# GateLoop and a low-rank mixer on one core: up products of two pairs ahead of the mix instead of one, with stacked float32r corrections

## The chip, the cores and the metric

The kernel runs on one core of a Trainium2 chip. The metric is the device time of one execution in microseconds (us): the median of several runs, and for the profile the time of the one execution that was profiled. TensorE is called PE, VectorE DVE, ScalarE ACT, GpSimd POOL and SyncE SP, as in the profile.

## The reference

```python
# attention: B, H, S, D = 4, 8, 768, 48; all inputs float32
for t in range(S):
    new_re = ar * S_re - ai * S_im          # ar, ai: the gate a[t], its magnitude cut at 0.999
    new_im = ar * S_im + ai * S_re
    S_re, S_im = new_re + k[t] (outer) v[t], new_im
    y[t] = q[t] @ S_re
x = y as (B, S, H * D)                      # (4, 768, 384)
# mixer: U (768, 32), V (32, 768), w_ch1 (384, 1536), w_ch2 (1536, 384)
h = x.transpose(0, 2, 1) @ U @ V            # a sum over the 768 tokens of a batch
u = x + h.transpose(0, 2, 1)                # "the mix"
out = u + relu(u @ w_ch1) @ w_ch2           # "up", then "down"
```

The weights of the mixer arrive as 64-bit floats and are converted on the chip.

## The kernel before, in words

**Work and order.** The 3072 tokens are 24 chunks of 128 tokens, six to a batch; two chunks are a pair, so there are 12 pairs (`m` = 0 to 11), three to a batch. Every operation is first entered in a plan (`PE(...)`, `ACT(...)`, `DVE(...)`, `POOL(...)`, `SP(...)`) with a planner's cost, what it reads and writes, and the buffers it takes. What is then issued is a list written out by hand or by a search, `ORDER`: the plan's operation numbers in one common order, from which each engine gets its own queue, in order. `SPARE` gives, for some operation numbers, how many dummy products PE makes just ahead of that operation (two records each). SP issues the loads and small transfers, POOL the stores of finished outputs and the carries between chunks.

**The chunks.** `gates` turns the gate inputs of two chunks at a time into magnitudes and angles (`magnitudes`, `turns`, `waves`; ACT and DVE, with prefix sums as PE products at lines 750 to 820). `prep` weighs q and k, forms the `QKC` tiles and transposes them on PE (line 881); `chain` makes a chunk's products (910, 930, 968, 960), carries the state `G` from chunk to chunk, and leaves the chunk's part of x in `xo`.

**The mixer of a pair.** The function `mixer(m)` does, when a batch is complete, the rank product `rank` (line 1003: x times U, summed over the six chunks, 32 columns wide, in four quarters of 96 columns on four groups of 32 partitions), its copy `r` (1009), and per pair: `spread` (line 1063: 16 tiled products with V on 32 rows each) and `mixed` (1070: four additions onto `xo`), `turned` (transposes of u), up, and down.

**Two forms of up.** `up_cut` is used from pair 1 on. Weights and inputs are cut into a high part and a low part (`cut_weights`, once; `turned`, per pair), and each block of outputs is made of three kinds of float32r products: high with high, low with low (lines 1148, 1150) and the crossed differences (1155), the last added by DVE (1169). `up` (line 1179) makes plain float32 products. It is used for pair 0 with `ahead`: that is, from x before the mix, as soon as the pair's two chunks are there. The part that the mix would have added is corrected later: `ranked` (line 1196) multiplies the transposed r with w_ch1 into `rws`, and `corrected` (lines 1214, 1220) multiplies that with V in tiles of 32 rows and adds it to h with the relu.

**Three forms of down.** `down` for pair 0 (line 1243), `down_two` for pairs 1 to 8 (line 1286; seven products instead of eight, each in two halves of three), `down_three` for the last three pairs (1463).

**Constants.** `AHEAD = 1` counts the pairs whose up is made ahead; `THREE = 9` and `PLAIN = 1` choose the forms of down. `weights` loads the weights in pieces of 768 KB through two staging buffers (`raw`); a piece below `EARLY` has its two conversions on DVE, a later one on ACT.

Of the kernel before, what the change touches and what calls it, by code (L numbers as in the profile page):

```python
# [10 lines left out]
FP = mybir.dt.float32  # L11
# [105 lines left out]
)  # L117

SPARE = {
    110: 8, 133: 7, 137: 2, 194: 3, 198: 2, 201: 3, 208: 1, 218: 5, 247: 5, 409: 2, 548: 1, 2206: 14,  # L120
}

DUMP = None
# [1562 lines left out]
```

## Time and profile before

| what | value |
|---|---|
| runs | 533.96, 535.43, 535.63 us; median 535.43 |
| the profiled execution | 535.18 us; its span from first to last instruction 533.3 us |
| granted PE clock | 1.0 throughout |
| PE busy | 511.0 us (96%) |
| DVE busy | 430.7 us (81%) |
| ACT busy | 310.5 us (58%) |
| DMA | 39.92 MB; mean 75 GB/s, 163 to 225 GB/s in the first seven of 40 slices of the span |

Busy time of PE is modelled from pipelined products, so a product that waits may look busy; "PEld", the loading of weights into PE, shows the gaps better. A line of the chain of waits reads: start in us, duration in us, engine, tile, line, number of instructions. A line of a group of instructions reads: line, engine, operation, output and inputs, shapes, count, then busy us and mean ns of one, then idle time of the engine ahead of them.

### The profile page before, as it was taken

What the parts mean: (1) busy time and instruction counts of PE and PEld (TensorE: products, weight loads), DVE (VectorE), ACT (ScalarE), POOL (GpSimd) and SP (SyncE); (2) the same over time, 40 slices, a digit from 0 to 9 for tenths busy, and PEclk for the clock granted to TensorE, in tenths of its full rate; (3) what the DMA queues carried; (4) which work ended last, traced back from release to release, by engine and by line L of the source; (5) the groups of instructions that cost most, each with busy time, mean ns of one, the idle gap of its engine ahead of it and who ended that gap; (6) DMA issues with size and microseconds to landing.
All of it is one profiled execution on the core that took longest, in us unless ns stands there. A gap on an engine that the chain in (4) does not pass through costs nothing.

```text
span 533.3 us, 17003 instructions
## 1 busy us (share of the span) xinstructions
PE 511.0 (96%) x7454; PEld 466.5 (87%) x7454; DVE 430.7 (81%) x798; ACT 310.5 (58%) x554; POOL 29.9 (6%) x57
## 2 busy tenths in 40 slices
PE   7789999899999998999999999999999999999996
PEld 7567686469999988999999989999999899999996
DVE  7998999999998976886977866786967758788741
ACT  6879999777587783655568764453475652321000
POOL 1000000000102000011002000011002000000020
PEclk9999999999999999999999999999999999999999
DMA  9996968430254442303217460024104300000011
GB/s 185 206 214 163 225 166 197 87 60 1 39 85 105 92 97 29 61 30 69 45 32 128 79 121 17 16 40 91 31 3 85 62 12 2 1 1 1 0 64 52
DMA packets 150704, 39.92 MB, mean 75 GB/s; under 512 B 145880, under 2 KB 147440, under 8 KB 150624
## 3 DMA queue, kind: packets, MB, share of 16 engines
q1 hardware_dynamic: 148544, 34.63, 33.1%
q0 software_dynamic: 2080, 4.15, 2.3%
q8 instruction: 59, 0.97, 0.8%
q14 instruction: 21, 0.17, 0.1%
HBM read 33.60 MB, written 4.76 MB: 72 GB/s over the span
## 4 chain that ended last, share of the span: by engine, by line
PE 79%; DVE 10%; ACT 6%; issue 2%; DMA 1%; SPq 0%; ACTq 0%; DVEq 0%
PE down L1286 20%; PE up L1148 8%; PE bank L1155 8%; PE up L1150 8%; PE bank L1463 7%; PE bank L910 4%; PE bank L881 4%; PE bank L968 4%; PE bank L930 3%; PE bank L960 3%; PE down L1243 2%; PE up L1179 2%; PE bank L1063 1%; PE bank L814 1%; DMA qk<-in_q_dram 1%
## 5 line engine op out<-in xcount | busy, mean ns | idle before, releaser
L1148 PE MATMUL up<-uh,wh 128*128 128x256 f32 x396 | 70.6, 287 | 0.1
L1150 PE MATMUL up<-ul,wl 128*128 128x256 f32 x396 | 68.5, 281 | 0.3 <-DVE ul L1107 0.3
L461 ACT ACTIVATE h<-up 128x512 f32<-128x512 f32 x60 | 35.2, 594 | 46.8 <-PE up L1150 46.3
L1148 PEld LDWEIGHTS up<-uh,wh 128*128 128x128 f32 x396 | 56.8, 189 | 1.2 <-ACT h L461 0.3
L1150 PEld LDWEIGHTS up<-ul,wl 128*128 128x128 f32 x396 | 56.2, 189 | 0.5 <-DVE ul L1107 0.5
L887 ACT COPY QK<-bank 112x512 f32<-112x512 f32 x96 | 51.2, 590 | 8.8 <-PE bank L881 8.6
L1155 PE MATMUL bank<-ud,wd 128*128 128x256 f32 x396 | 55.2, 283 | 0.0
L1286 PE MATMUL down<-w,h 128*128 128x192 f32 x288 | 53.6, 331 | 0.2
L1155 PEld LDWEIGHTS bank<-ud,wd 128*128 128x128 f32 x396 | 50.7, 188 | 0.2
L464 DVE TENSOR_TENSOR QKC<-qk,cs 128x768 f32<-128x768 f32 x48 | 44.9, 955 | 5.8 <-ACT cs L461 4.0
L1286 PEld LDWEIGHTS down<-w,h 128*128 128x128 f32 x288 | 46.6, 190 | 1.5 <-DVE h L1169 0.4
L467 DVE TENSOR_TENSOR xo<-bank,xo 128x192 f32<-128x192 f32 x78 | 26.1, 354 | 24.3 <-PE bank L1463 17.5
L1169 DVE CUSTOM_DVE_ANT_0 h<-bank,h 128x512 f32<-128x512 f32 x54 | 35.8, 687 | 10.2 <-PE bank L1155 8.1
L1286 PE MATMUL down<-stage 128*128 128x192 f32 x192 | 35.7, 333 | 0.5 <-issue 0.3
L800 POOL DMA_DIRECT2D z<-F x15 | 12.1, 806 | 376.1 <-ACT z L461 102.9
L1286 PEld LDWEIGHTS down<-stage 128*128 128x128 f32 x192 | 31.0, 190 | 1.6 <-issue 0.4
L458 ACT ACT_TABLE_LOAD x24 | 30.8, 1283 | 1.1 <-PEq L1670 0.7
L881 PE MATMUL bank<-ident,QKC 64*112 64x64 f32 x768 | 28.5, 220 | 2.4 <-DVE QKC L464 1.7
L881 PEld LDWEIGHTS bank<-ident,QKC 64*112 64x112 f32 x768 | 24.1, 130 | 7.5 <-issue 2.6
L1106 ACT CAST uh<-low 128x384 fp32r<-128x384 f32 x22 | 11.2, 509 | 31.2 <-DVE low L1104 26.6
L910 PE MATMUL bank<-QK 112*64 112x64 f32 x768 | 27.6, 225 | 0.6 <-ACT QK L887 0.6
L910 PEld LDWEIGHTS bank<-QK 112*64 112x64 f32 x768 | 24.3, 138 | 3.9 <-issue 1.7
(234 smaller groups left out, 1066.4 us busy)
## 6 DMA issues: line engine op xcount, KB each, us to landing
stage<-in_moe_w_ch_dram SPq DMA_DIRECT2D x12, 768.0 KB
qk<-in_q_dram SPq DMA_DIRECT2D x24, 192.0 KB
qk<-in_k_dram SPq DMA_DIRECT2D x24, 192.0 KB
values<-in_v_dram SPq DMA_DIRECT2D x24, 192.0 KB
gate<-in_a_re_dram SPq DMA_DIRECT2D x22, 192.0 KB
gate<-in_a_im_dram SPq DMA_DIRECT2D x22, 192.0 KB
out_dram<-xo POOLq DMA_DIRECT2D x13, 192.0 KB, 3.0
out_dram<-xo POOLq DMA_DIRECT2D x16, 96.0 KB, 3.1
```

Of the source, the lines that this page charges most:

```text
L458: ACT(1.4, rank, lambda: nc.scalar.preload_act_table_set(name), writes=[TABLE])
L461: return nc.scalar.activation(out=o, in_=i, func=f, **kw)
L464: nc.vector.tensor_tensor(out=o, in0=a, in1=b, op=OP.mult)
L881: nc.tensor.transpose(out=get(*ps[r])[0:DQ, h], in_=get(*qkc)[at, h].rearrange("p u d -> p (u d)")[:, 0:DQ], identity=ident[at, at], tile_ ...
L887: nc.scalar.copy(out=get(*QK)[0:DQ, u].rearrange("p (h t) -> p h t", t=CH)[:, :, r * HC:(r + 1) * HC], in_=get(*ps[r])[0:DQ])
L910: nc.tensor.matmul(out=get(*ps0)[r:r + HC, h], lhsT=k_of(h, r, HC), rhs=q_of(h, r, HC), start=True, stop=True, tile_position=(0, r))
L1148: nc.tensor.matmul(out=get(*X)[:, e], lhsT=get("wh", f)[:, at(e)], rhs=get(*uh)[:, f], start=(f == 0), stop=False)
L1150: nc.tensor.matmul(out=get(*X)[:, e], lhsT=wl_of(f)[:, at(e)], rhs=get(*ul)[:, f], start=False, stop=(f == KD - 1))
L1155: nc.tensor.matmul(out=get(*Y)[:, e], lhsT=wd[:, f, at(e)], rhs=get(*ud)[:, f], start=(f == 0), stop=(f == KD - 1))
L1169: DVE(c_dve(2 * N), R0, lambda: nc.vector._custom_dve(dve_ops.TENSOR_ADD_SAT, out=where_(), in0=get(*Y), in1=where_(), s0=math.inf, s1=0.0 ...
L1286: nc.tensor.matmul(out=get(*to)[:, part], lhsT=x(j), rhs=y[:, j], start=(first and j == 0), stop=(j == KH - 1), skip_group_check=not first)
L1463: nc.tensor.matmul(out=get(*ps), lhsT=w[0]()[:, q], rhs=x[0]()[:, q], start=(n == 0 and q == 0), stop=(q == k3 - 1), skip_group_check=True)
```

## The change

**Pairs.** `AHEAD` becomes 2 and a new constant `CUTS = 2` says from which pair on up is made in the cut form. Pairs 0 and 1 both get plain float32 up products from x before the mix, and corrections. `cut_weights` and `turned` in its cut form come in with pair 2. h of pair 0 takes the space that later holds the low weights (`wl`), h of pair 1 the usual one; the tiles `wd` and V share their space in time with the new operands.

**Stacked corrections.** V is held a second time as `V4`, a float32r tile of 128 rows: four copies of its 32 rows, of which the second and the fourth hold what float32r rounding left over. r is sent to DRAM and back into four places of 32 partitions (`low`), with all 384 columns, and made into `R4`: the first two groups rounded, the last two the remainder. One product of 128 rows then gives the sum of four partial products. `spread` becomes one float32r product of 384 columns for each chunk, `mixed` one addition of 384 columns. In the same way `rws` goes to DRAM and back and becomes `rw4`, and `corrected` becomes two float32r products and one addition of 512 columns for each two blocks of h, six times a pair.

**The rest.** U and V are loaded as the sixth piece instead of the third, and the pieces with conversions on DVE are 0, 3, 4, 5 and 6; `QKC` loses its gap between the two halves' paddings; the five constant columns share one tile; from batch 1 on, r's quarters are cut as contiguous columns. `ORDER` is another list (2231 operations instead of 2208), and `SPARE` has 74 dummy products instead of 53.

In the new order, read as operations: 6 of the 12 halves of pair 0's up and one of pair 1's stand ahead of batch 0's last rank product on PE (before: 11 of pair 0's), the other 17 behind it; 11 half products of pair 2's down stand behind batch 1's rank product (before: 3). On SP, r's first store stands behind a weight piece and a load, and the twelve loads of r (three for each of four places in batch 0, one for each place later), the store and four loads of `rws` follow behind a load and the last weight piece.

The diff, cut to its core (the two lists are left out):

```diff
-    SINGLE, AHEAD = 3, 1
+    SINGLE, AHEAD, CUTS = 3, 2, 2
-    EARLY, SPREAD = 6, (0, 1, 2)
+    EARLY, SPREAD = (0, 3, 4, 5, 6), (0, 1, 2)
...
+    buffer(("rwf", 0), "wd0", 1, [128, FF])
+    buffer(("wdx", 0), "wd0", 1, [128, FF], dtype=FR)
+    buffer(("rw4", 0), "wd1", 1, [128, FF], dtype=FR)
...
+    V4 = singles.tile([128, S], FR, name="V4")
+    R4 = singles.tile([128, DM], FR, name="R4")
...
+                    ACT(c_act(S), ("w1", p), lambda: nc.scalar.copy(out=V4, in_=get("V", 0)), [("V", 0)], [("V4", 0)])
+                    for n in range(1, NP, 2):
+                        at = slice(n * R, (n + 1) * R)
+                        DVE(c_dve(S), ("w1", p), lambda at=at: nc.vector.tensor_tensor(
+                            out=V4[at], in0=get("V", 0)[at], in1=V4[at].bitcast(FP), op=OP.subtract), [("V", 0)], [("V4", 0, at.start)])
...
+            SP(0.3, ("load", 7), lambda: nc.sync.dma_start(out=get(*rd), in_=get(*r)), [r], [rd])
+            for n in range(NP):
+                def spread_r(n=n):
+                    x = get(*rd).rearrange("(n r) c -> r n c", r=R)
+                    o = low[n * R:(n + 1) * R]
+                    if b:
+                        nc.sync.dma_start(out=o.rearrange("r (n c) -> r n c", n=NP), in_=x)
+                    else:
+                        for f in range(KD):
+                            nc.sync.dma_start(out=o[:, f * 128:(f + 1) * 128].rearrange("r (n t) -> r n t", t=R), in_=x[:, :, f * R:(f + 1) * R])
+                SP(0.3, ("load", 7), spread_r, [rd], [("low", 0, n)])
+            ACT(c_act(DM), R0, lambda: nc.scalar.copy(out=R4, in_=low), [("low", 0)], [("R4", 0)])
+            DVE(c_dve(DM), R0, lambda: nc.vector.tensor_tensor(
+                out=R4[2 * R:], in0=low[2 * R:], in1=R4[2 * R:].bitcast(FP), op=OP.subtract), [("low", 0)], [("R4", 0)])
...
-                        nc.tensor.matmul(out=get(*ps[n])[:, cc], lhsT=V[at, c * CH:(c + 1) * CH],
-                                         rhs=get(*r)[at], start=True, stop=True, tile_position=(n * R, 0))
+                PE(0.18, R0, lambda cc=cc, at=at: nc.tensor.matmul(out=get(*ps[cc]), lhsT=V4[:, at], rhs=R4, start=True, stop=True),
+                   [("R4", 0), ("V4", 0)], [ps[cc]], steps=1)
...
+            SP(0.3, ("load", 7), lambda: nc.sync.dma_start(out=get(*rd), in_=rws), [rw], [rd])
+            for n in range(NP):
+                SP(0.3, ("load", 7), lambda n=n: nc.sync.dma_start(
+                    out=get(*rf)[n * R:(n + 1) * R].rearrange("r (x n t) -> r x n t", n=NP, x=NR),
+                    in_=get(*rd).rearrange("(n r) (x t) -> r x n t", r=R, x=NR)), [rd], [rf + (n,)])
...
+                for e in range(2):
+                    nc.tensor.matmul(out=get(*ps)[:, e], lhsT=get("rw4", 0)[:, (ff + e) * 128:(ff + e + 1) * 128],
+                                     rhs=V4[:, c0 * CH:c0 * CH + N], start=True, stop=True)
+            PE(0.24, RM, products, [("rw4", 0, ff * 128 // WP), ("V4", 0)], [ps], steps=2)
...
-            for ff in range(0, NP, 2):
+            for ff in range(0, KF, 2):
                 corrected(ff)
...
-        if m >= AHEAD:
-            if m == AHEAD:
+        if m >= CUTS:
+            if m == CUTS:
                 cut_weights()
```

More of the change, by code (lines that the diff above doesn't have):

```diff
@@ L375 @@
     WP = 768
+    EDGES = (0, 768, 1536)
     fast = ExitStack()
@@ L501, with wd_of @@
     F = singles.tile([128, GC, DM], FP, name="F")
-    wd = singles.tile([128, KD, FF], FR, name="wd")
-    wl = singles.tile([128, KD - 1, FF], FR, name="wl")
+    buffer(("rwf", 0), "wd0", 1, [128, FF])
+    buffer(("wdx", 0), "wd0", 1, [128, FF], dtype=FR)
+    buffer(("rw4", 0), "wd1", 1, [128, FF], dtype=FR)
+    buffer(("wdx", 1), "wd1", 1, [128, FF], dtype=FR)
+    buffer(("V", 0), "last", 1, [128, S], padded=[128, FF])
+    buffer(("wdx", 2), "last", 1, [128, FF], dtype=FR)
+    def wd_of(f):
+        return get("wdx", f)
     for f in range(KD):
@@ L509, with column @@
     U = UV[:, 0:NCH * R].rearrange("p (c r) -> p c r", r=R)
-    V = singles.tile([128, S], FP, name="V")
-    def column(nm, value):
-        t = singles.tile([128, 1], FP, name=nm)
+    V4 = singles.tile([128, S], FR, name="V4")
+    R4 = singles.tile([128, DM], FR, name="R4")
+    columns = singles.tile([128, 5], FP, name="columns")
+    def column(n, value):
+        t = columns[:, n:n + 1]
         nc.vector.memset(t, value)
@@ L541 @@
     for n in range(NQ):
-        QKC.append(singles.tile([128, H, 2, DP], FP, name="QKC%d" % n))
-        nc.gpsimd.memset(QKC[n][:, :, :, D:DP], 0.0)
+        QKC.append(singles.tile([128, H, DQ], FP, name="QKC%d" % n))
+        nc.gpsimd.memset(QKC[n][:, :, D:DP], 0.0)
     GATE = singles.tile([128, 3, GC * DM], FP, name="gate")
@@ L626, in tokens, with w1_names @@
         return a.rearrange("(c p) m -> p c m", p=128)
+    def w1_names(f, lo, hi):
+        return [("w1", f, a) for a, b in zip(EDGES, EDGES[1:]) if a < hi and b > lo]
     ALL_W2 = [("w2", f) for f in range(0, KF, 2)]
@@ L632, in weights @@
         p = 0
-        for h in range(0, FF, WP):
+        for h, e in zip(EDGES, EDGES[1:]):
             for f in range(KD):
-                if p == 2:
+                if p == 5:
                     single(p, ("w1", p), ("UV", 0), UV, [tokens(moe_U), tokens(moe_V.rearrange("r (s m) -> (r s) m", m=m))])
@@ L850, in wl2, with parts_of @@
         return T["wl2",]
+    def parts_of(a):
+        x = a[:, :, 0:D]
+        return bass.AP(x.tensor, x.offset, [x.ap[0], x.ap[1], (DP, 2), x.ap[2]])
     def T_of(i):
@@ L1008, in mixer @@
                    [sums_r + (("k", cs[0] - 1),)] * (cs[0] > 0), [sums_r + (("k", c),) for c in cs], steps=2 * NP * len(cs))
-            ACT(c_act(RC), R0, lambda: nc.scalar.copy(out=get(*r), in_=get(*sums_r)), [sums_r], [r])
+            ACT(c_act(RC), R0, lambda: nc.scalar.copy(out=get(*r), in_=get(*sums_r)), [sums_r], [r] + [("prefix_z", 0)] * (b == 0))
+            rd = ("RD", b)
+            buffer(rd, "RD", 2, [128, RC], bass.MemoryType.DRAM)
+            SP(0.3, ("load", 7), lambda: nc.sync.dma_start(out=get(*rd), in_=get(*r)), [r], [rd])
[12 more added lines that the diff above has]
+                out=R4[2 * R:], in0=low[2 * R:], in1=R4[2 * R:].bitcast(FP), op=OP.subtract), [("low", 0)], [("R4", 0)])
         uT, h = ("uT", m), ("h", m)
@@ L1055, in spread, with mixed @@
         def spread():
-            ps = [out_of("mixed", (m, n), [128, MC, RC], [128, 512 // RC // MC * MC, RC]) for n in range(NP)]
-            def products():
-                for cc in range(MC):
-                    for n in range(NP):
-                        at, c = slice(n * R, (n + 1) * R), c0 + cc
-                        nc.tensor.matmul(out=get(*ps[n])[:, cc], lhsT=V[at, c * CH:(c + 1) * CH],
-                                         rhs=get(*r)[at], start=True, stop=True, tile_position=(n * R, 0))
-            PE(0.45, R0, products, [r, ("V", 0)], ps, way=4, steps=4 * NP)
-            return ps
-        def mixed(n, ps):
-            u = XO[i0 // MC % len(XO)].rearrange("p c (f n t) -> p n c f t", n=NP, t=R)[:, n]
-            DVE(c_dve(MC * RC), R0, lambda: add(u, get(*ps)[:, 0:MC].rearrange("p c (f t) -> p c f t", t=R), u), [ps],
-                [("xo", i0 + cc) for cc in range(MC)])
+            ps = [out_of("mixed", (m, cc), [128, DM], [128, 512]) for cc in range(MC)]
+            for cc in range(MC):
+                at = slice((c0 + cc) * CH, (c0 + cc + 1) * CH)
+                PE(0.18, R0, lambda cc=cc, at=at: nc.tensor.matmul(out=get(*ps[cc]), lhsT=V4[:, at], rhs=R4, start=True, stop=True),
+                   [("R4", 0), ("V4", 0)], [ps[cc]], steps=1)
+            return ps
+        def mixed(cc, ps):
+            DVE(c_dve(DM), R0, lambda: add(get("xo", i0 + cc), get(*ps), get("xo", i0 + cc)), [ps], [("xo", i0 + cc)])
         def turned():
@@ L1084, in turned @@
             PE(0.39, R0, turn, us, tr, way=5, steps=2 * KD * MC)
-            if ahead:
+            if m < CUTS:
                 for r in range(2):
@@ L1154, in crosses @@
                     for f in range(KD):
-                        nc.tensor.matmul(out=get(*Y)[:, e], lhsT=wd[:, f, at(e)], rhs=get(*ud)[:, f], start=(f == 0), stop=(f == KD - 1))
+                        nc.tensor.matmul(out=get(*Y)[:, e], lhsT=wd_of(f)[:, at(e)], rhs=get(*ud)[:, f], start=(f == 0), stop=(f == KD - 1))
             low_w = [("wl", f, y) for f in range(KD - 1)] + [("wl2", y)]
@@ L1166, in up_cut @@
                    takes=[to] if to in plan.tag else [], steps=2 * KD)
-            PE(0.655, RM, crosses, [ud] + [("wd", f, y) for f in range(KD)], [Y], steps=2 * KD)
+            PE(0.655, RM, crosses, [ud] + [("wd", f, y) for f in range(KD)], [Y], takes=[("wdx", f) for f in range(KD)], steps=2 * KD)
             ACT(c_act(2 * N) - 0.045, R0, lambda: act(where_(), get(*X), AF.Copy, scale=1.0 + 1.0 / SHIFT), [X], [part] + own)
@@ L1181, in up @@
             for es in ((0,), (1,)) if ahead else ((0, 1),):
-                PE(1.295 * len(es), RM, lambda es=es: products(es), [uT] + [("w1", f, lo) for f in range(KD)], [ps + (e,) for e in es], takes=[h],
+                PE(1.295 * len(es), RM, lambda es=es: products(es), [uT] + [n for f in range(KD) for n in w1_names(f, (ff + es[0]) * 128, (ff + es[-1] + 1) * 128)],
+                   [ps + (e,) for e in es], takes=[h],
                    steps=2 * KD * len(es))
@@ L1200, in ranked @@
             ACT(c_act(NR * 128) - 0.05, R0, lambda: nc.scalar.copy(out=rws.rearrange("p (x t) -> p x t", t=128), in_=get(*ps)), [ps], [rw])
-        def corrected(ff):
-            e = [f for f in range(2 * NP) if f % NP in (ff, ff + 1)] + [2 * NP + ff, 2 * NP + ff + 1]
-            pairs = [[f for f in e if f % NP == n and f < 2 * NP] for n in (ff, ff + 1)], [[e[-2]], [e[-1]]]
-            for ks in pairs:
-                tiles = [(k, out_of("fix", (m, k[0]), [128, len(k), N], [128, 2, N])) for k in ks]
-                def products(tiles=tiles):
-                    for y in range(len(tiles[0][0])):
-                        for k, ps in tiles:
-                            n, to = k[y] % NP, k[y] // NP * 128
-                            at = slice(n * R, (n + 1) * R)
-                            nc.tensor.matmul(out=get(*ps)[:, y], lhsT=rws[at, to:to + 128], rhs=V[at, c0 * CH:c0 * CH + N],
-                                             start=True, stop=True, tile_position=(n * R, 0))
-                PE(0.6 * len(ks[0]), RM, products, [("s2", 0, 1), ("V", 0)] + [h + (f // 2 * 2,) for k in ks for f in k],
-                   [ps for k, ps in tiles], way=4, steps=4 * len(ks[0]))
-                for k, ps in tiles:
-                    o = lambda k=k: get(*h)[:, k[0]:k[-1] + 1:NP]
-                    DVE(c_dve(len(k) * N), R0, lambda o=o, ps=ps: nc.vector._custom_dve(
-                        dve_ops.TENSOR_ADD_SAT, out=o(), in0=get(*ps), in1=o(), s0=math.inf, s1=0.0), [ps],
-                        [h + (f // 2 * 2, "x%d" % f) for f in k])
@@ new lines, in ranked, with products @@
+            for y in range(2):
+                at = slice(y * WP, (y + 1) * WP)
+                ACT(c_act(WP), R0, lambda at=at: nc.scalar.copy(out=get(*r4)[:, at], in_=get(*rf)[:, at]), [rf], [r4 + (y,)])
+                DVE(c_dve(WP), R0, lambda at=at: nc.vector.tensor_tensor(
+                    out=get(*r4)[2 * R:, at], in0=get(*rf)[2 * R:, at], in1=get(*r4)[2 * R:, at].bitcast(FP), op=OP.subtract), [rf], [r4 + (y,)])
+        def corrected(ff):
+            ps = out_of("fix", (m, ff), [128, 2, N], [128, 2, N])
+            def products():
+                for e in range(2):
+                    nc.tensor.matmul(out=get(*ps)[:, e], lhsT=get("rw4", 0)[:, (ff + e) * 128:(ff + e + 1) * 128],
+                                     rhs=V4[:, c0 * CH:c0 * CH + N], start=True, stop=True)
+            PE(0.24, RM, products, [("rw4", 0, ff * 128 // WP), ("V4", 0)], [ps], steps=2)
+            o = lambda: get(*h)[:, ff:ff + 2]
+            DVE(c_dve(2 * N), R0, lambda: nc.vector._custom_dve(
+                dve_ops.TENSOR_ADD_SAT, out=o(), in0=get(*ps), in1=o(), s0=math.inf, s1=0.0), [ps], [h + (ff,)])
@@ L1503, in mixer @@
             turned()
-        if m >= AHEAD:
-            if m == AHEAD:
+        if AHEAD <= m < CUTS:
+            for ff in range(0, KF, 2):
+                up(ff)
+        if m >= CUTS:
+            if m == CUTS:
                 cut_weights()
```

46 lines of the change are left out of this document (25 added, 21 removed), and 171 rows, old and new, of the table ORDER.

## Prediction

> **What bounds the kernel now.** I read the page's first part, then busy time by stage, then the chain of waits in order of time, then instructions and waits where the change acts. First the page, then five stages cut where the last sum over tokens of batch 0 (its rank product, line 1003) ends, where pair 1's up products end, at chunk 7, where batch 1's rank product begins, and the rest:
>
> ```profile
> span 533.3 us, 17003 instructions
> PE 511.0 (96%) x7454; PEld 466.5 (87%) x7454; DVE 430.7 (81%) x798; ACT 310.5 (58%) x554; POOL 29.9 (6%) x57
> ```
> ```profile
> core 0: us, PE busy (x) PEld busy (x) DVE busy (x) ACT busy (x) POOL busy (x), PEclk, DMA share, GB/s
> 0.00:85.10 85.10, 74.77 (x1378) 60.14 (x1378) 77.83 (x143) 73.38 (x130) 1.68 (x13) 1.00 0.87 192
> 85.10:130.70 45.60, 42.22 (x296) 29.82 (x288) 44.84 (x77) 35.15 (x51) 0.96 (x1) 1.00 0.40 81
> 130.70:160.90 30.20, 29.86 (x509) 27.90 (x508) 28.84 (x53) 20.58 (x37) 2.68 (x4) 1.00 0.33 55
> 160.90:203.80 42.90, 41.22 (x892) 38.27 (x884) 36.31 (x63) 32.46 (x63) 3.24 (x5) 1.00 0.52 100
> 203.80:533.30 329.50, 322.92 (x4399) 310.38 (x4398) 242.86 (x465) 148.94 (x275) 21.32 (x34) 1.00 0.21 42
> ```
>
> The mean (PE 96%) hides three regimes. Behind 203.8 PE is busy 322.92 of 329.5 us: TensorE bounds, and each us of its work is a us of the kernel. From 85.1 to 160.9 DVE is busy 44.84 + 28.84 = 73.7 of 75.8 us (2.1 idle): DVE bounds, and PE's "busy" is padded by waiting matmuls (PEld is 29.82 of 45.6). Before 85.1 DVE and ACT are both near nine tenths full. The chain of waits shows who is late:
>
> ```profile
> 53.07 5.71 DMA qk<-in_q_dram
> ...
> 63.81 2.59 PE up L1179 x12
> ...
> 77.22 2.80 PE up L1179 x12
> ...
> 144.90 3.91 PE down L1286 x24
> ...
> 338.67 2.15 PE bank L1155 x18
> ```
>
> At 63.8 and 77.2 pairs of halves of pair 0's up stand in the chain, the later ones between chunks 4 and 5, ahead of batch 0's last sum. Behind that sum PE's instructions show it waiting for DVE, which corrects h while it also cuts the weights:
>
> ```profile
> 87.53 0.34 PE L750 MATMUL bank<-gs,prefix_r 128*128 128x384 f32 x1
> 87.71 0.34 PE L750 MATMUL bank<-GS,prefix_r 128*128 128x384 f32 x1
> ...
> 92.17 1.16 PE L1214 MATMUL bank<-V,stage 32*128 32x256 f32 x16
> ...
> 98.17 0.70 PE L1214 MATMUL bank<-V,stage 32*128 32x256 f32 x4 [1.36 <-DVE h L1220]
> ...
> 115.27 0.70 PE L1063 MATMUL bank<-r,V 32*128 32x96 f32 x16
> 115.90 0.62 PE L1148 MATMUL up<-uh,wh 128*128 128x256 f32 x3
> ```
>
> **The sum on TensorE.** Pair 1 leaves the cut form: 36 x 3 fp32r products, each 2.15/18 = 0.119 us, so -12.9. It gains 36 fp32 products; a half (3 of them, 6 records) takes 2.59/2 = 1.295, 12 halves +15.5. The spread products of a pair take 115.90 - 115.27 = 0.63 now; the two stacked 384-wide fp32r ones go at 87.71 - 87.53 = 0.18 each: -0.27 a pair, -3.2 over 12. The old corrections, 24 tiled records, took about 1.16 + 2 x 0.70 = 2.6; the new ones are 24 fp32r products at 0.119, 2.8. Sum: -12.9 + 15.5 - 3.2 + 0.2 = -0.4 us. TensorE's work hardly changes; the time can only come from where the work stands, which the two orders tell when their numbers are read as operations.
>
> [...]
>
> **Stage 1, to the end of batch 0's rank product (85.1 us).** Before, 11 of 12 halves of pair 0's up stand ahead of it; after, 6, and one half and the transposes (0.5) of pair 1. So PE has 5 x 1.295 - 1.8 = 4.7 us less in front, and the 2.80 at 77.2 is gone from between chunks 4 and 5. Late next is ACT: two more weight conversions (1.069 + 0.940), pair 1's copy of its transposes (0.5), less two copies of h (2 x 0.594): +1.3 of work in an engine that idles 11.7 of 85.1 us.
>
> ```profile
> L461 ACT ACTIVATE stage<-stage 128x768 uint16<-128x768 uint32 x7 | 7.5, 1069 | 0.0
> L461 ACT ACTIVATE w<-stage 128x768 f32<-128x768 f32 x7 | 6.6, 940 | 0.0
> L461 ACT ACTIVATE h<-up 128x512 f32<-128x512 f32 x60 | 35.2, 594 | 46.8 <-PE up L1150 46.3 <-PE up L1179 0.4
> ```
>
> I take -2.0: the 2.80 less some 0.8 of ACT's 1.3. Bounds: -4 (all of 4.7 but the transposes' share) and +3, since 21 more dummy products (0.22 each, 4.6 us) are put where PE is expected to wait; they cost nothing only in those gaps. The later U and V, the moved weight pieces, the packed QKC and the constants in one tile lie under DVE and ACT here: nothing, at most the +3.
>
> **Stage 2, rank product to rank product (118.7 us now).** DVE works 44.84 + 28.84 + 36.31 = 110.0 of it. Its edits, by width:
>
> ```profile
> L467 DVE TENSOR_TENSOR xo<-bank,xo 128x192 f32<-128x192 f32 x78 | 26.1, 354 | 24.3 <-PE bank L1463 17.5 <-PE bank L1063 4.6 <-issue 2.1
> L1220 DVE CUSTOM_DVE_ANT_0 h<-bank,h 128x256 f32<-128x256 f32 x4 | 1.7, 425 | 0.0
> L467 DVE TENSOR_TENSOR xo<-down,xo 128x384 f32<-128x384 f32 x10 | 5.5, 555 | 1.3 <-PE down L1286 1.3
> L1169 DVE CUSTOM_DVE_ANT_0 h<-bank,h 128x512 f32<-128x512 f32 x54 | 35.8, 687 | 10.2 <-PE bank L1155 8.1 <-ACT h L461 1.2 <-ACT cs L461 0.8
> L1130 DVE TENSOR_TENSOR wd<-wl,wt 128x768 fp32r<-128x768 f32 x6 | 5.8, 960 | 0.0
> ```
>
> Mixes of three pairs: 3 x (2 x 0.555 - 4 x 0.354) = -0.9. Cutting pair 1's inputs goes (4 x 0.555 + 0.960): -3.2; its six adds: -4.1. Corrections: 12 x 0.687 - 4 x 0.687 - 4 x 0.425 = +3.8. V4's and the corrections' low halves, 4 x 0.960, and r's, 0.555: +4.4. One cut of weights comes in from stage 1 (half a 0.960 form): +0.5. Moved behind batch 1's rank product: six sums (0.555), four adds (0.354) of pair 2 and one weighing (0.960): -5.7. Together -5.2: 104.8. The cutting of the weights itself (18 DVE operations) only moves from before pair 1's up to before pair 2's, inside the stage. So DVE still bounds it. PE fills underneath, with no more to do than now: 16 halves of up come in (+20.7), the cut form and its transposes (-13.4), three spreads less the corrections (-0.6) and eight half products of pair 2 (0.977, -7.8) go out. To 104.8 add the way from the last DVE operation to the rank product, 3 us, an idle of 2.1 as in 85.1 to 160.9, and the wait for the new trips through DRAM.
>
> ```profile
> L768 SPq DMA_DIRECT2D T<-TD x24: 321/522/2448, 25.2 to 409.2; - x24
> L639 SPq DMA_DIRECT2D V<-UV x4: 602/646/884, 53.6 to 78.1; - x4
> SPq L768 <- DMA TD<-es: 7.5, 5, 2.8
> z<-F POOLq DMA_DIRECT2D x15, 1.5 KB, 1.9
> out_dram<-xo POOLq DMA_DIRECT2D x16, 96.0 KB, 3.1
> ```
>
> r goes out and comes back on SP, the queue of the loads: the store waits for r, then a q/k load and the last weight piece are issued, then twelve loads of r (three for each of four places), the store and four loads of the corrections' weights; four input loads of later groups queue behind. With r copied at +1.2 us, a store of 2.2 (between 1.9 and 2.8), twelve issues at 0.522 (T's loads, the nearest: small pieces from DRAM), a landing of 1.9, copy and subtraction 0.5 + 0.555, the operand is there at +12.7. PE's cover to the first spread product is 0.7 + 2.1 + 5 x 1.295 + 0.4 = 9.7 us; DVE and ACT stand at the same operand with about as much in front. Wait: 3.0. Stage 2: 104.8 + 3 + 2.1 + 3.0 = 112.9, -5.8. Bounds: 109 (-9.7, no wait, 1 idle) and 122 (+3).
>
> **Stage 3, to the end (PE-bound).** Behind batch 1's rank product now stand 11 instead of 3 half products of pair 2's down (3.91/4 = 0.977 each): +7.8; nine spreads -2.4: +5.4. They cover the trip of r there (four loads, 7.6 us in all, against 7 x 0.977 + 0.7). If they don't, up to 2 us for each of three batches. Bounds +4 and +11.
>
> Sum: -2.0 - 5.8 + 5.4 = -2.4 against the profiled execution's 535.18 us (span 533.3 and 1.9 around it; the median of the runs, 535.43, is 0.25 above): 532.8 us.
>
> **Rivals.** *The trips stop all three engines (slower).* A row speaks for it: the q load at 53.07 took 5.71 us, because a 768 KB piece had been issued just ahead:
>
> ```profile
> 52.66 0.37 SPq L602 DMA_DIRECT2D stage<-in_moe_w_ch_dram  x1
> ```
>
> In the new order r's store follows such a piece and a load. At 5.7 for the store, V's 0.646 per issue and 3.1 for the landing the operand comes at 1.2 + 5.7 + 7.8 + 3.1 + 1.1 = 18.9, 9.2 late instead of 3.0; the second trip, queued behind, adds some 1.5. That is +7.7: 540.5. It turns slower by 0.3% once the waits exceed 3.0 + 4.0 = 7.0. Against it: the piece may have drained by then, and T's loads mostly issue faster than V's. [...] Chance 0.33, with the later batches' trips (537 to 541).
>
> *Stage 1 gains nothing*, as ACT's extra 1.3 and the dummies eat the freed PE time: -0.4, 534.8, no change that can be told. For it: DVE 77.83 and ACT 73.38 of 85.1. Chance 0.23.
>
> **How the numbers follow.** The forecast, 532.8, with its neighbours from 526 to 533.5, has 0.44 (the low end: -4 - 9.7 + 4 with all bounds, -9.7, is 525.5). The range 526 to 541 leaves out what lies under the forecast's low bounds and above the slow rival, under 2 in 10. About 0.3% (1.6 us) is what a measurement of this kernel can tell from no change: faster 0.44, within 0.23, slower 0.33.
>
> **What would show it.** In the profile after: batch 0's last rank product ends near 83, batch 1's begins near 196; PE idle or waiting before the first spread product about 3 us, released by the subtraction on DVE or by the DMA; DVE still full in between; the half of an up product still 1.295; the half products of pair 2's down behind batch 1's rank without a gap. Wrong would be: a wait at r's operand over 7 us, DVE falling under nine tenths in stage 2, a gap behind the later rank products, or batch 0's rank product behind 86.

## The result, and the profile after

The changed kernel takes 554.28 us (median of four runs, 552.08 to 555.70) against 534.69 us for the kernel before on the same chip (four runs, 533.35 to 535.63): a ratio of 1.0331, 95% interval [1.0283, 1.0380]. The change makes the kernel 19.6 us slower. The forecast was 532.8 us, 1.9 faster, with a range of 526 to 541; the measured time lies 13 above that range.

The profiled execution took 553.08 us; its page begins:

```profile
span 550.8 us, 16731 instructions
PE 520.1 (94%) x7292; PEld 476.8 (87%) x7292; DVE 434.5 (79%) x774; ACT 314.7 (57%) x562; POOL 29.8 (5%) x57
...
PEclk9999999899779999999999999999999999999999
```

The three stages of the prediction's sum, cut at the end of batch 0's rank product and at the start of batch 1's, from the view that gives busy time by stretch (start:end, length, busy PE, PEld, DVE, ACT, POOL with instruction counts, granted clock, DMA share, GB/s):

```profile
0.00:84.60 84.60, 75.69 (x1409) 61.59 (x1409) 75.93 (x140) 74.81 (x132) 1.77 (x13) 1.00 0.89 200
84.60:216.30 131.70, 115.93 (x1567) 97.37 (x1567) 108.54 (x175) 90.65 (x154) 6.82 (x10) 0.94 0.40 75
216.30:550.80 334.50, 328.51 (x4321) 317.84 (x4320) 250.01 (x460) 149.21 (x277) 21.21 (x34) 1.00 0.23 45
```

Stage 1 took 84.6 us (85.1 before), stage 3 334.5 (329.5). Stage 2 took 131.7 instead of 118.7. So 13.0 of the 17.5 us by which the spans differ lie between the two rank products, and the granted clock, 1.00 throughout before, is 0.94 there. PE's instructions of that stage show where it stood (start, duration, line, operation; in brackets the idle time ahead and what ended it):

```profile
97.17 0.97 PE L1105 MATMUL bank<-R,V 128*128 128x384 f32 x4 [2.46 <-DVE R L1052]
...
105.15 1.21 PE L1258 MATMUL bank<-V,rw 128*128 128x256 f32 x8 [3.12 <-DVE rw L1249]
...
134.29 6.72 PE L1284 MATMUL down<-w,h 128*128 128x384 f32 x20
150.49 0.69 PE L838 MATMUL bank<-GS,prefix_r 128*128 128x384 f32 x1 [9.48 <-DVE GS L832]
```

Three stalls: 2.46 us at the first spread product (r's trip through DRAM), 3.12 at the first correction (the trip of its weights), 9.48 behind pair 0's last down product. The product at 150.49 belongs to an angle and has nothing to do with the mixer; it stands behind a queue. ACT's wait, and the DVE instruction that ends the idle time on DVE, show which queue:

```profile
ACT wlx L463 <- PE down L1284: 12.7, 1, 12.7
```

```profile
142.66 1.82 DVE L1169 TENSOR_TENSOR wdx<-wlx,wt 128x768 fp32r<-128x768 f32 x2 [10.09 <-ACT wlx L463]
```

ACT waits 12.7 us to write the first low half of the cut weights (`wlx`), until the last down product of pair 0 (line 1284) is done. The two share no data, but memory: pair 0's h lies in `"wl"`, the place of the low halves (lines 1085 and 1088). Behind `wlx` in ACT's queue stand an angle and copies of q and k, behind `wdx` in DVE's the sums that the angle of the next chunk needs. PE, once it has ended the down products, waits for those.

SP shows a longer wait that looks like a cause, and isn't (e2 below): a q load stands 26.6 us, and from 108 to 131 us the view by stretch has a DMA share of 0.00.

```profile
SPq L597 <- DVE GS L832: 26.6, 1, 26.6
```

The stalls cost more than their length. The clock around them:

```profile
105.00:106.00 1.00, 0.85 (x7) 0.85 (x8) 0.93 (x4) 0.98 (x2) 0.00 (x0) 1.00 0.26 45
106.00:107.00 1.00, 0.94 (x7) 0.67 (x6) 1.00 (x2) 0.99 (x2) 0.00 (x0) 0.86 0.85 170
107.00:110.00 3.00, 3.00 (x10) 2.46 (x9) 2.96 (x6) 2.85 (x5) 0.00 (x0) 0.50 0.00 1
...
141.00:144.00 3.00, 0.01 (x1) 0.00 (x0) 1.34 (x2) 2.95 (x5) 0.00 (x0) 1.00 0.06 9
144.00:145.00 1.00, 0.00 (x0) 0.00 (x0) 0.48 (x1) 1.00 (x3) 0.00 (x0) 0.64 0.00 0
145.00:157.00 12.00, 6.26 (x103) 5.33 (x104) 12.00 (x20) 8.47 (x12) 0.75 (x1) 0.50 0.17 33
157.00:158.00 1.00, 1.00 (x11) 0.56 (x11) 1.00 (x3) 0.39 (x1) 0.00 (x0) 0.54 0.75 148
```

About 3.3 us into the long gap the granted clock is halved, and PE works at the halved clock for some 7 us after the gap has ended (150.5 to 157.9).

### The profile page after: what moved, and what is told of

It is laid out like the page before. It is cut to its first block, busy times and chain, and to the rows that moved or that the text cites. A ratio compares the mean times of both kernels' runs of the same rounds, so it can differ in the third digit from the quotient of the medians.

```text
span 550.8 us, 16731 instructions
## 1 busy us (share of the span) xinstructions
PE 520.1 (94%) x7292; PEld 476.8 (87%) x7292; DVE 434.5 (79%) x774; ACT 314.7 (57%) x562; POOL 29.8 (5%) x57
## 4 chain that ended last, share of the span: by engine, by line
PE 77%; ACT 5%; DMA 3%; DVE 2%; issue 1%; SPq 1%; ACTq 0%
PE down L1327 21%; PE up L1187 8%; PE bank L1194 8%; PE up L1189 8%; PE bank L1504 7%; PE bank L938 4%; PE bank L909 4%; PE bank L996 3%; PE down L1284 3%; PE bank L958 3%; PE up L1216 2%; PE bank L988 2%; DMA stage<-in_moe_w_ch_dram 2%; PE bank L838 1%; PE bank L774 1%; ACT QK L915 1%
## 5 line engine op out<-in xcount | busy, mean ns | idle before, releaser
L1187 PE MATMUL up<-uh,wh 128*128 128x256 f32 x360 | 64.9, 289 | 0.0
L1194 PE MATMUL bank<-ud,wdx 128*128 128x256 f32 x360 | 51.1, 285 | 0.0
L1189 PE MATMUL up<-ul,wlx 128*128 128x256 f32 x240 | 48.3, 283 | 0.0
L1194 PEld LDWEIGHTS bank<-ud,wdx 128*128 128x128 f32 x360 | 46.4, 191 | 0.8 <-DVE h L1208 0.3
L1189 PEld LDWEIGHTS up<-ul,wlx 128*128 128x128 f32 x240 | 37.3, 191 | 0.0
L469 DVE TENSOR_TENSOR xo<-bank,xo 128x192 f32<-128x192 f32 (+1 forms) x54 | 22.5, 441 | 18.3 <-PE bank L1504 15.9
L1216 PE MATMUL up<-uT,w 128*128 128x256 f32 x144 | 34.9, 394 | 0.2 <-DVE uT L1127 0.2
L1189 PE MATMUL up<-ul,wl 128*128 128x256 f32 x120 | 33.9, 282 | 0.0
L469 DVE TENSOR_TENSOR xo<-down,xo 128x192 f32<-128x192 f32 (+1 forms) x58 | 22.2, 386 | 13.4 <-PE down L1327 13.3
L1216 PEld LDWEIGHTS up<-uT,w 128*128 128x128 f32 x144 | 27.6, 197 | 4.8 <-ACT es L463 0.6
```

Source lines behind the costliest of these rows:

```text
L469: nc.vector.tensor_tensor(out=o, in0=a, in1=b, op=OP.add)
L1187: nc.tensor.matmul(out=get(*X)[:, e], lhsT=get("wh", f)[:, at(e)], rhs=get(*uh)[:, f], start=(f == 0), stop=False)
L1189: nc.tensor.matmul(out=get(*X)[:, e], lhsT=wl_of(f)[:, at(e)], rhs=get(*ul)[:, f], start=False, stop=(f == KD - 1))
L1194: nc.tensor.matmul(out=get(*Y)[:, e], lhsT=wd_of(f)[:, at(e)], rhs=get(*ud)[:, f], start=(f == 0), stop=(f == KD - 1))
L1216: nc.tensor.matmul(out=get(*ps)[:, e], lhsT=get("w1", f)[:, (ff + e) * 128:(ff + e + 1) * 128], rhs=get(*uT)[:, f], start=(f == 0), stop=( ...
```

## The experiments

Twelve kernels. Times are medians; the ratio is to the kernel before, timed beside it (534.69 us for the changed kernel, 535.85 to 536.52 for e1 to e12). Stage ends come from the rank products' rows: stage 1 ends with the start of batch 0's last one, stage 2 with the start of batch 1's first, and stage 3 is the rest of the span. They come from one profile a kernel, and some 2.5 us in a stage can be chance: stage 1 is 86.9 in e3 and 86.8 in e9, whose edits act only behind it.

| kernel | us | ratio, 95% interval | stage 1 | stage 2 | stage 3 |
|---|---|---|---|---|---|
| before | 534.69 | 1 | 85.0 | 118.8 | 329.5 |
| changed | 554.28 | 1.0331 [1.0283, 1.0380] | 84.3 | 132.0 | 334.5 |
| e1_rw_act | 553.84 | 1.0331 [1.0304, 1.0358] | 85.0 | 133.5 | 336.5 |
| e2_swap | 545.13 | 1.0187 [1.0156, 1.0218] | 84.5 | 122.7 | 333.7 |
| e3_dummies | 556.98 | 1.0406 [1.0364, 1.0449] | 86.9 | 134.1 | 334.2 |
| e4_behind | 546.38 | 1.0204 [1.0153, 1.0255] | 84.3 | 125.6 | 335.6 |
| e5_no_trips | 546.59 | 1.0186 [1.0138, 1.0234] | 84.1 | 125.5 | 335.9 |
| e6_swap_no_trips | 539.76 | 1.0069 [1.0043, 1.0095] | 85.3 | 118.2 | 334.2 |
| e7_swap_order | 552.97 | 1.0335 [1.0289, 1.0381] | 88.0 | 123.2 | 337.8 |
| e8_order | 551.87 | 1.0295 [1.0254, 1.0336] | 88.7 | 123.8 | 335.1 |
| e9_four_loads | 550.59 | 1.0245 [1.0181, 1.0309] | 86.8 | 129.1 | 333.1 |
| e10_few_dummies | 553.16 | 1.0321 [1.0247, 1.0394] | 85.0 | 130.4 | 335.7 |
| e11_swap_four | 543.01 | 1.0139 [1.0063, 1.0215] | 84.7 | 120.8 | 335.0 |
| e12_order_again | 538.42 | 1.0054 [1.0031, 1.0077] | 84.0 | 117.2 | 334.8 |

The rows behind the first two and the last line of the table:

```profile
L1003 PE MATMUL bank<-xo,UV x144: 245/246/270, 203.8 to 439.0; 128*32 128x96 f32 x144
L1003 PE MATMUL rank<-xo,UV x48: 245/246/271, 83.4 to 85.0; 128*32 128x96 f32 x48
```

```profile
L1031 PE MATMUL bank<-xo,UV x144: 246/246/270, 216.3 to 447.9; 128*32 128x96 f32 x144
L1031 PE MATMUL rank<-xo,UV x48: 246/258/270, 54.1 to 84.3; 128*32 128x96 f32 x48
```

```profile
L1034 PE MATMUL bank<-xo,UV x144: 246/246/270, 201.2 to 432.6; 128*32 128x96 f32 x144
L1034 PE MATMUL rank<-xo,UV x48: 246/258/270, 54.1 to 84.0; 128*32 128x96 f32 x48
```

**e2: other memory for the low halves.**

```
-    buffer(("wdx", 1), "wd1", ...)          +    buffer(("wla", 1), "wd1", ...)
-    buffer(("wdx", 2), "last", ...)         +    buffer(("wla", 0), "last", ...)
-    buffer(("wlx", 0), "wl", 1, [128, KD - 1, FF], dtype=FR)
+    buffer(("wdy", 0), "wl", 1, [128, KD - 1, FF], dtype=FR)
...                                               # the uses follow the new names
```

> The changed kernel in its own order; only memory is exchanged: the low halves of cut weights of two row blocks lie where V and the corrections' weights lay (free by 125 us), and two of the differences lie in their place, in the memory that pair 0's h holds until its last down product. Theory (memory): ScalarE's wait of 12.7 us before the first low half goes, VectorE's 10.1 goes for the most part, TensorE's gap at 141 shrinks from 9.5 to about 4 and the low clock behind it shortens: 545 to 549. Rival (SP's queue: loads blocked from 105 to 131 us by a q load that waits): gap and time stay, 553 to 555.

Stage 2 lost 9.3 us, the run 1.4% (some 8 us). The gap, and the clock behind it:

```profile
142.78 0.44 PE L841 MATMUL bank<-GS,prefix_r 128*128 128x384 f32 x1 [3.06 <-DVE GS L835]
```

```profile
142.80:144.00 1.20, 0.70 (x2) 0.35 (x2) 1.20 (x3) 1.20 (x3) 0.00 (x0) 1.00 0.00 0
144.00:145.00 1.00, 1.00 (x46) 0.92 (x48) 1.00 (x4) 0.54 (x1) 0.00 (x0) 0.54 0.00 0
145.00:147.00 2.00, 2.00 (x60) 1.91 (x54) 2.00 (x3) 1.91 (x3) 0.00 (x0) 0.50 0.40 77
147.00:148.00 1.00, 1.00 (x13) 0.88 (x12) 1.00 (x3) 0.14 (x1) 0.00 (x0) 0.75 0.28 58
```

```profile
SPq L600 <- DVE GS L835: 26.3, 1, 26.3
```

The gap fell from 9.48 to 3.06 us and the half clock behind it from 7 to 3.4 us, while the q load on SP still waits 26.3 us. The memory was the cause; SP's wait cost nothing that shows. In the kernels that keep the memory and the order around it, e1, e5, e9 and e10, the gap is 9.48 us each time. What is left of it in e2 has the same source, since two of the differences (`wdy`) now lie where pair 0's h was, and DVE waits there for the same down products:

```profile
139.76 0.96 DVE L1172 TENSOR_TENSOR wdy<-wla,wt 128x768 fp32r<-128x768 f32 x1 [4.01 <-PE down L1287]
```

**e4: the same memory, the queue behind the wait.**

```
-    478, 724, 544, 548, 723, 554, 550, 711, 732, ...
+    478, 724, 723, 711, 732, 736, 731, 735, 712, 713, 488, 499, 500, 753, 714, 501, 715, 544, ...
```

> The changed kernel with fifteen operations taken ahead of the first low half of the cut weights: on ScalarE six (the next angles and copies of q and k), on VectorE eight, and a POOL transfer; all had their inputs before the wait. Memory as in the changed kernel. Theory (memory, and who queues behind the wait): the wait of ScalarE and VectorE shortens but its start is still the last down product of pair 0; TensorE's gap at 141 falls from 9.5 to about 6.5 and moves to another product: 548 to 551. Rival (SP's queue): 553 to 555.

The time fell by 1.3%, more than expected. The first fence is e4, the second the changed kernel:

```profile
140.94 0.94 PE L958 MATMUL bank<-values,QKC 64*48 64x48 f32 x64
141.80 1.15 PE L938 MATMUL bank<-QK 112*64 112x64 f32 x32
147.06 2.29 PE L1327 MATMUL down<-w,h 128*128 128x192 f32 x6 [4.10 <-DVE xo L469]
```

```profile
152.04 1.53 PE L958 MATMUL bank<-values,QKC 64*48 64x48 f32 x64
153.51 1.97 PE L938 MATMUL bank<-QK 112*64 112x64 f32 x32
```

The same 96 products took 3.50 us behind the changed kernel's gap and 2.09 here, ahead of one. So e4 gained the gap's difference (9.48 to 4.10) and part of the clock. What stood behind the wait cost the time, as much as the wait itself.

**e5, e6: the trips taken away,** alone and with e2. Both make the operand and the weights from a constant column:

```
-  SP(... nc.sync.dma_start(out=get(*rd), in_=rws) ...)      +  SP(... None ...)      # and the loads
-  nc.scalar.copy(out=get(*r4)[:, at], in_=get(*rf)[:, at])
+  nc.scalar.copy(out=get(*r4)[:, at], in_=ident[:, 0:1].to_broadcast([128, WP]))
```

> The changed kernel without the two trips of batch 0 through DRAM: the store and twelve loads of r, the store and four loads of the corrections' weights are left out, and r's operand and the corrections' weights are made, by the same ScalarE and VectorE operations, from a constant that is always there (so batch 0's low-rank term is not the reference's). Theory (each wait at a trip's operand is lost time): TensorE's waits of 2.5 and 3.1 us go, the low clock of 104 to 112 with them, the later gap of 9.5 comes as much earlier: 5.6 to 6.6 less, 547 to 549. Rival (VectorE's work bounds the stage, and it catches up behind the waits): 1 to 3 less, 551 to 553.

> The exchange of memory and the missing trips together (batch 0's low-rank term is not the reference's). Theory (two independent losses, the memory of pair 0's h 7.7 to 8.5 us with its clock, the trips 5.6): 538.5 to 540.5; what then stays above the kernel before, 3 to 5 us, is the shorter gap at the cut, and the last stage's 5 us against the one gained. Rival (both waits are for the same VectorE work, so only the larger counts): 544 to 546.

e5: 1.4% less, stage 2 6.5 us shorter: a little more than 2.46 + 3.12. e6: stage 2 13.8 us shorter than in the changed kernel, where the two alone gave 9.3 + 6.5 = 15.8. As far as one profile each can tell, the two losses are nearly independent, and together they are the whole excess of stage 2: 118.2 us, as before (118.8).

**e1, e9: why the trips are late.** e1 sends the second trip through ACT's queue, e9 fetches r with four loads:

```
-  SP(0.3, ("load", 7), lambda: nc.sync.dma_start(out=get(*rd), in_=rws), ...)
+  plan.add("ACT", 0.4, ("load", 7), lambda: nc.scalar.dma_start(out=get(*rd), in_=rws), ...)     # and the loads
```

```
-  for f in range(KD):
-      nc.sync.dma_start(out=o[:, f * 128:(f + 1) * 128].rearrange("r (n t) -> r n t", t=R), in_=x[:, :, f * R:(f + 1) * R])
+  nc.sync.dma_start(out=o.rearrange("r (f n t) -> r f n t", n=NP, t=R), in_=get(*rd).rearrange("(n r) (f t) -> r f n t", r=R, t=R))
```

> The changed kernel, with the second trip (store and four loads of the corrections' weights) issued by ScalarE's queue right behind the copy that makes them, instead of by SP behind r's twelve loads. Theory (queue place): the trip is late because SP issues it at 94.5, 5 us after its data stand; from ScalarE it lands by about 98, TensorE's wait of 3.1 us before the first correction goes, and with it the low clock (0.84, 0.73) of 104 to 112 us: 549.5 to 551 instead of 554.3. Rival (the landing itself is slow, 4.6 us from DRAM): the operand comes 1 to 2 us earlier at most, 552 to 554. The later gap of 9.5 us at 141 stays in both.

> The changed kernel with r of batch 0 brought back by four loads instead of twelve, each over all three column blocks; the pieces in DRAM and in memory are the same (1536 of 128 bytes). Theory (the trips are late by what SP spends on issuing, 7.2 us for twelve): the issue falls to about 2.4, r's operand comes 4 to 5 us sooner, the store behind it too, both of TensorE's waits (2.5 and 3.1) go: 546.5 to 549.5, as without the trips. Rival (the pieces set the time, not the loads): the issue of one load takes three times as long, nothing changes: 552.5 to 555.

e1 gained nothing. Its issues on ACT (duration in ns: least, median, most; first and last start in us), then ACT and PE:

```profile
L1243 ACTq DMA_DIRECT2D rwf<-RW x4: 564/598/687, 93.6 to 99.1; - x4
...
99.86 0.51 ACT L1051 CAST R<-low 128x384 fp32r<-128x384 f32 x1 [5.52 <-DMA TD<-es]
```

```profile
101.02 1.65 PE L1105 MATMUL bank<-R,V 128*128 128x384 f32 x4 [5.19 <-DVE R L1052]
```

The second wait is gone and the first is 5.19 instead of 2.46. An issue took ACT as long as SP, about 0.6 us (SP's four loads in the changed kernel: 2.63 together), but on ACT the four stretch from 93.6 to 99.7, with pauses of 2.46 us behind the second and 1.13 behind the third. The chain of waits ends the later pause with the landing of a gate load that SP had issued; what ended the first isn't shown. The copy of r stands behind the last issue in ACT's queue and starts 0.2 us after it. So an issue was hardly shorter on ACT, and ACT's own work behind the issues paid for the move.

e9, the issues of r's trip in the changed kernel (the first fence, with SP's wait among them) and in e9, with the landing of the last load from the chain of waits, then e9's PE:

```profile
87.18 7.22 SPq L1049 DMA_DIRECT2D low<-RD  x12
94.50 0.37 SPq L1241 DMA_DIRECT2D RW<-stage  x1
...
96.59 2.63 SPq L1243 DMA_DIRECT2D rwf<-RW  x4
...
SPq L1049 <- DMA stage<-in_moe_w_ch_dram: 1.8, 1, 1.8
```

```profile
89.68 2.63 SPq L1048 DMA_DIRECT2D low<-RD  x4
92.41 0.55 SPq L1240 DMA_DIRECT2D RW<-stage  x1
...
97.32 2.58 SPq L1242 DMA_DIRECT2D rwf<-RW  x4
...
91.69 5.05 DMA low<-RD
```

```profile
98.00 0.97 PE L1104 MATMUL bank<-R,V 128*128 128x384 f32 x4 [0.76 <-DVE R L1051]
105.65 1.20 PE L1257 MATMUL bank<-V,rw 128*128 128x256 f32 x8 [2.80 <-DVE rw L1248]
```

The issue fell from 7.22 to 2.63 us. Two things went: the twelve loads took a median of 0.43 us each, the four, with three times the pieces, 0.62; and among the twelve SP stood 1.8 us until the 768 KB weight piece that it had issued just ahead had landed. So the issue goes mostly by loads. But the first wait fell only by 1.7 us, to 0.76, because the last load now lands 5.05 us after its issue; in the changed kernel ACT starts on r 2.0 us after the last load's (93.97 to 96.02). The second stayed at 2.80: its store left 4.6 us earlier relative to r's first load, but a gate load and two small stores stand between it and its loads (93.01 to 96.31 on SP; the loads are issued from 97.32 to 99.90), and these bring 4 x 192 KB, as much as a piece of the weights; how much of the wait is due to either was not shown. Half the theory held: the time lies between its range and the rival's, and the gain of 0.9% is inside overlapping intervals. With e2 (e11, 543.01 us) the time again lies between the two ranges; the gain on e2 is 0.5%, inside the intervals.

> The exchange of memory and the four loads together. If the four loads take away the waits at the trips: 538.5 to 541, as the kernel without the trips. If the pieces set the trip's time: 544 to 546, as the exchange alone.

**e3, e10: dummy products.** Only the table of counts changes (`494: 9, 485: 12, 716: 40` added; for e10 all but `113: 8, 465: 3, 2229: 12` taken out).

> The changed kernel with 61 small dummy products more, in TensorE's three gaps: 9 before the first spread product, 12 before the first correction, 40 before the product at which TensorE stood 9.5 us. Nothing else changes. Theory (the gaps cost twice: themselves, and the clock behind them): the granted clock stays at 1.00 from 104 to 112 and from 144 to 159 us, the gaps stay as long as they were, and the time falls by what the low clock cost, 3 to 4.6 us: 549.5 to 551.5. Rival (the clock falls for another reason, or its fall costs nothing since TensorE isn't the bound there): 553 to 555, or up to 1 more.

> The changed kernel with 42 fewer dummy products (of 78) in the first stage, from the start to 85 us; nothing else changes. Theory (the dummies stand in gaps and cost nothing): batch 0's last rank product stays at 84 to 85, the time at 553 to 555. Rival (they and ScalarE's load ate the time that the moved up products freed): the product comes 1 to 2 us earlier, and so does the end: 551.5 to 553. A third way: without them the granted clock falls in that stage and it ends later, 555 to 559.

e3 got slower, and its second half tested nothing:

```profile
107.81 1.21 PE L1258 MATMUL bank<-V,rw 128*128 128x256 f32 x8 [1.27 <-DVE rw L1249]
...
148.23 11.05 PE L1658 MATMUL bank<-ident 128*128 128x128 f32 x80 [5.20 <-DVE h L1262]
```

The dummies of the long gap write the bank of the product that they precede; the bank came free only 5.2 us into the gap, when the clock was already halved, and they ran on for 11.05 us. The first half worked, the clock stays at 1.00:

```profile
108.00:112.00 4.00, 3.94 (x23) 3.41 (x23) 3.92 (x8) 3.84 (x5) 0.00 (x0) 1.00 0.01 2
```

From the first correction to the end of pair 0's down it took 35.2 us instead of 35.9, so that clock fall had cost about 0.7 us.

e10's edit takes out 51 of the 74 dummy products (its expectation counted 42 of 78). It has the clock at half for part of stage 1 and the same time:

```profile
20.00:30.00 10.00, 6.13 (x140) 5.59 (x142) 9.12 (x14) 9.38 (x15) 0.00 (x0) 0.50 0.95 216
```

Fewer dummies and a lower clock together change nothing that can be measured there, where DVE and ACT are nearly full. The run doesn't tell dummies that cost nothing from a cost that the lower clock made up.

**e7, e8, e12: other orders.** Nothing but `ORDER` (with e2 in e7, with e2 and e9 in e12). In e7 one dummy product falls on a part of one up sum of pair 1, which therefore isn't the reference's.

> The exchange of memory, and another order of the operations up to 225 us: work that doesn't depend on r stands ahead of the products that wait for the trips, and the angles and copies ahead of the cuts that wait for pair 0's h. Theory (waits, not work, lost the time): no gap over 3 us on TensorE behind batch 0's last sum, granted clock 1.00, batch 1's rank product near 198 instead of 216: 531 to 537. Rival (the landing of the trips and VectorE's work bound it, whatever the order): 541 to 546.

> Another order alone, memory as in the changed kernel: the low halves still wait for pair 0's last down product, but that product stands earlier, and other work stands in the wait. Theory (the order decides what the shared memory costs): 533 to 539, within 3 us of the kernel with the exchange. Rival (shared memory costs its 8 us in any order): 541 to 546.

> The exchange of memory, the four loads, and another order of the operations from batch 0's last rank product to about 150 us; the first stage and what follows stay in their order. Up products stand where TensorE waited for the corrections' weights, angles and copies where it waited for the cut. Theory (waits lost the time, so that without them the stage is as short as the forecast had it): no gap over 2 us on TensorE from 85 to 205, granted clock 1.00, batch 1's rank product 118 to 120 us behind batch 0's or sooner, end at 534 to 538, at or just above the kernel before. Rival (with the waits gone TensorE is itself the bound, and the last stage's 5 us stay): 538 to 542.

e7 and e8 missed both of their ranges: they had no PE gap over 2.5 us behind batch 0's sum and their stage 2 is 8 to 9 us shorter than the changed kernel's, but their order also touches stage 1, which got 4 us longer and had less behind it (1330 and 1372 PE instructions by 85 us, against 1410). e12 leaves stage 1 alone. It has no gap over 0.81 us from 85 to 205, the clock is 1.00, and stage 2 is the shortest of all, here from the end of one rank product to the start of the next:

```profile
84.30:201.20 116.90, 113.69 (x1568) 93.74 (x1568) 109.68 (x177) 91.14 (x154) 6.85 (x10) 1.00 0.41 81
```

Still 538.42, 0.54% [0.31, 0.77] above the kernel before. What the theory said of the gaps, the clock and the stage came true, but the time lies just inside the rival's range. None of the twelve beats the kernel before.

## Why the prediction was wrong, step by step

- **Stage 1, -2.0 forecast:** -0.5 to -0.7 measured, within the bounds. The rival "stage 1 gains nothing" had this right for the stage; which of its reasons holds stays open. e10, with fewer dummies and a lower clock, ends the stage no earlier (85.0).
- **Stage 2, -5.8 forecast, bounds -9.7 and +3:** +13.0. The step that failed is "The cutting of the weights itself (18 DVE operations) only moves from before pair 1's up to before pair 2's, inside the stage." The cut was counted as VectorE work and moved at no cost, although the change puts pair 0's h into the memory that the cut writes. A buffer that is taken over is a wait like any other, with a queue behind it: 12.7 us on ACT, 9.48 on PE, and 7 us of half clock. e2 and e4, which undo the one or the other end of it, each won back 7 to 8 us. Of the prediction's own signs of being wrong, DVE under nine tenths in stage 2 is the one that came: 108.54 of 131.7 us.
- **r's trip, 3.0 forecast:** 2.46. The operand was expected at +12.7 and was there at +12.5 (97.1 against 84.6). That is close in part by luck: the loads began at +2.6 and not +3.4, and took 7.22 us and not 6.3. The price of an issue was too high (0.522 a load; the median is 0.43), and the 1.8 us in which SP stood until the weight piece had landed had no term in the sum.
- **The second trip, nothing forecast, 1.5 in the slow rival:** 3.12. The prediction counted its four issues, and not that they bring 768 KB. The DMA share is 1.32 at 189 GB/s from 100 to 104 us, and the chain of waits has the landing of the last one, 4.58 us from its issue:

```profile
98.59 4.58 DMA rwf<-RW
```

- **The rival "the trips stop all three engines", 540.5:** right in sign, but smaller. The weight piece ahead did hold SP, for 1.8 us, in the middle of the twelve loads and not at the store. PE's waits were 2.5 and 3.1 us (6.5 us of stage 2 by e5) where it had 9.2 and 1.5. It explains less than half of the result; the larger part no rival named.
- **"DVE still bounds" stage 2:** the second step that failed. PE's busy 113.3 of 118.7 us was read as padded by waiting products, because PEld was low. But PEld is as low where no wait of PE shows: in the changed kernel's last down products of pair 0, while DVE and ACT stand idle:

```profile
136.00:140.00 4.00, 4.00 (x14) 2.40 (x13) 0.00 (x0) 0.00 (x0) 0.00 (x0) 1.00 0.86 148
```

  The kernel before makes 48 products of the same form from 94 to 115 us, inside the stage that was read as padded. e12 leaves no wait over 0.81 us, and its 116.9 us between the rank products hold 113.69 us of PE and 109.68 of DVE; the forecast had 109.9 us for the stage without the wait for r. So, as far as busy times can show it, both engines were nearly full and there was little to win: the stage gains 1.6 us in e12, not 8.8. DVE's own sum was also off (108.5 measured in the changed kernel, 104.8 forecast). Another order could be shorter than e12's; that wasn't shown.
- **Stage 3, +5.4 forecast:** +5.0, and 3.6 to 8.3 in all other runs. This step was right: PE's busy time of the stage grows by 5.6 us (328.51 against 322.92), and no gap stands in front of the half products of pair 2 that move behind batch 1's rank product.
- **PE's work, -0.4:** busy 517.7 in e12 against 511.0, of which the 21 dummies account for 5.5 (24.4 against 18.9 over their groups); the rest, 1.3, is 1.7 us over the forecast. The spreads gave back 1.0 of busy time and not 3.2; from start to start, as the forecast counts, it is 2.3 in e12 (7.6 us before, 5.2 after), since several of them take about 0.3 us to the next start and not 0.18. The 24 products of the corrections are busy for 5.5 us in e12, where 2.8 was forecast. The spreads before and in the changed kernel:

```profile
L1063 PE MATMUL bank<-r,V 32*128 32x96 f32 x192 | 8.4, 289 | 0.4 <-ACT r L1009 0.4
```

```profile
L1105 PE MATMUL bank<-R,V 128*128 128x384 f32 x24 | 7.4, 380 | 2.5 <-DVE R L1052 2.5
```

The balance of e12 shows what is left of the change without any of its waits: -1.0 in stage 1, -1.6 in stage 2, +5.3 in stage 3, +2.7 for the span (536.0 against 533.3).

## What to carry to other kernels

When a change shares one memory between two tiles, find the last reader of the old one and the first writer of the new one, and cost that wait with everything that stands behind the writer in its engine's queue; here PE paid 9.48 us at an angle that has nothing to do with either. Before calling one engine the bound of a stage, take the other's busy time at its word until a run shows that it is padded. Cost a transfer by its landing as well as by its issues (the four loads of `rws` took 2.63 us to issue, and the last landed 4.58 us from its issue), and look at what was issued just ahead of it (here a weight piece that held SP for 1.8 us).

## What the hardware showed that was not expected

- PE gaps of 2.80 us (e9), 3.06 (e2) and 3.12 (the changed kernel at 102 to 105) were each followed by half clock. The length of one gap doesn't decide alone: behind 2.46 us (the changed kernel at 94.7) the clock stayed at 1.00, and behind 2.04 in e8 (145.2 to 147.3) it fell (0.78 from 145 to 150, 0.53 from 150 to 155). Behind the first three it began 1.3 to 2.1 us after the gap had ended and lasted 3.4 us; in the gap of 9.48 us it began after 3.3 us and lasted 13.6. In the changed kernel the changes keep a step: read in windows of 0.1 us, its clock changes at 106.73, 110.14, 144.27 and 157.93, which is 1, 10 and 4 times 3.41 us from one to the next.
- What half clock cost differed: 96 products took 3.50 us instead of 2.09 behind the long gap, the stretch behind the trips lost about 0.7 us (e3), and e10, with fewer dummies too, shows no difference.
- Issues stood until an earlier transfer had landed: SP 1.8 us among twelve loads behind a 768 KB piece (the changed kernel), ACT 1.13 us ahead of its fourth load until a gate load had landed (e1). On ACT, the engine's own work stood with them: the copy of r began at 99.86, 0.2 us after the last issue (e1).
